# x of block 3 on loaded channel by channel: an element-wise DMA in place of transposes on TensorE

## The chip, the core and the metric

The kernel runs on one core of a Trainium2 chip. A core has TensorE (PE, the matrix engine), VectorE (DVE), ScalarE (ACT), GpSimd (POOL) and SyncE (SP, which here only issues DMAs); each runs its own instruction list in order, and they wait for one another by semaphores. Sixteen DMA engines move data between the device memory and the on-chip memory SBUF. PE writes its results to PSUM. The metric is the device time of one execution in microseconds.

## The reference

The input x has 2 x 4096 tokens of 192 channels. Three steps follow one another, and only the last result is written out.

```python
# 1: causal convolution over 7 tokens, taps = softmax(weight), one set for each of 8 heads of 24 channels
out = np.einsum('hk,bskhg->bshg', w, x_unf)          # 8192 x 192
# 2: MLP with a sigmoid GELU, 192 -> 2048 -> 192
h = x @ w_in
g = h * (1.0 / (1.0 + np.exp(-1.702 * h)))
x = g @ w_out
# 3: MLP with a rational function, 192 -> 2048 -> 192
h = x @ w_in
P = a[0] + a[1] * h + a[2] * h**2 + a[3] * h**3
Q = 1.0 + np.abs(b[0]) * np.abs(h) + np.abs(b[1]) * h**2
return (P / (Q + 1e-06)) @ w_out
```

## The kernel before

The 8192 tokens are worked on in 16 blocks of T = 512 tokens. All activations stand transposed, with channels on partitions and tokens along the free axis. Channels 0 to 127 take a block of 128 x 512; channels 128 to 191 are folded: the first 256 tokens of a block on partitions 0 to 63, the other 256 on partitions 64 to 127, in a block of 128 x 256.

A stage j overlaps three blocks: the third step of block j, the second step of block j + 1, and the preparation (convolution) of block `conv` = j + 3. Each stage has a front and a back. In the front, `front_groups` makes sixteen products of 128 hidden units each in groups of three on PE (`h_group`, lines L420 and L434); ACT reads them from PSUM (L524 is the GELU, L585 and L586 start the polynomial), VectorE goes on (L587, L588, L593, L607, and L538 for the low half of a split). L588 is the operation that lets go of a product's PSUM tile. The ring of PSUM tiles for products has three places. In the back, `back_phase` runs the second projection of block j + 1 (`o1_product`, L496 and L506), then a maximum, scales and the first products of the next front, while ACT takes logarithms and sigmoids of block j.

x comes in through three functions. `x_load` reads the rows of a block as they lie in memory, tokens on partitions, into the tile `xn` (L245, L248). `x_halo` reads the six tokens ahead of the block, element by element, straight into the transposed tile `xt` (L261 to L263). `x_transpose` turns `xn` on PE in six transposes into a PSUM tile (L272), and ACT copies that into `xt` (L278, L279). `x_red` takes the largest absolute value of `xn` on VectorE (L370), from which a power-of-two scale is made. `x_conv_pool` then convolves on POOL: seven multiplies of each part (L328) and six adds (L332). Blocks 0, 1 and 2 are prepared in a prologue and in stage 0, with the convolution as matmuls on PE; blocks 3 to 15 go by way of `back_phase` and POOL, one in each of the stages 0 to 12.

The order on each engine is that of the program text. In the front, `extras[i]` is a list of steps that are appended behind unit i; `x_red(conv)` stands in `extras[2]`, the store of block j - 1 (L626 on ACT, L630 on SP) in `extras[6]`. Since SP works in order, the loads of the next stage go out right behind that store. The scales of the third step are four tiny POOL operations (`x2_scales`, L573) that stand behind the convolution in POOL's queue, and L585 of the next front needs them. L223 copies split weights from one half of the partitions to the other, in the prologue.

Of the kernel before, what the change touches and what calls it, by code (L numbers as in the profile page):

```python
# [13 lines left out]
ALU = mybir.AluOpType  # L14
AX = mybir.AxisListType
P = 128
# [4 lines left out]
def kernel(  # L21
# [12 lines left out]
    nc = tc.nc  # L34
    B, S, D = x.shape
# [4 lines left out]
    T = 512  # L40
# [3 lines left out]
    NG = T // P  # L44
    D2 = D - P
    HALO = K - 1
    TH = T // 2
    W = T + TH
    xf = x.rearrange("b s d -> (b s) d")
# [24 lines left out]
    def ps_tile(name):  # L74
        return ps_hs[-1].tile([P, 2, 512], F32, tag="h", name=name)
# [7 lines left out]
    def all_max(red, pm):  # L83

        nc.tensor.transpose(out=pm[:, 0, 0:P], in_=red.to_broadcast([P, P]), identity=ident)
# [153 lines left out]
    xn_t, xt_t, xc_t, xs_t = {}, {}, {}, {}  # L239

    def x_load(n):

        t = p2.tile([P, W], F32, tag="xn", name="xn")
        src = xf[n * T:(n + 1) * T].rearrange("(g p) d -> p g d", p=P)
        nc.sync.dma_start(out=t[:, 0:T].rearrange("p (g d) -> p g d", g=NG), in_=src[:, :, 0:P])  # L245
        side = t[:, T:W].rearrange("p (g h d) -> p g h d", g=2, h=2)
        for h in range(2):
            nc.sync.dma_start(out=side[:, :, h], in_=src[:, 2 * h:2 * h + 2, P:D])  # L248
        xn_t[n] = t

    def x_halo(n, t=None):
# [11 lines left out]
        nc.sync.dma_start(out=t[D2:P, 0:HALO], in_=xf[first + TH - HALO:first + TH, P:D].rearrange("s d -> d s"))  # L263
        xt_t[n] = t

    def x_transpose(n):

        pt = ps_tile("pt")
        src, t = xn_t.pop(n), xt_t[n]

        def turn(dst, c):
            nc.tensor.transpose(out=dst, in_=src[:, c:c + P], identity=ident)  # L272

        for g in range(2):
            turn(pt[:, 1, g * P:(g + 1) * P], T + g * P)
        for g in range(NG):
            turn(pt[:, 0, g * P:(g + 1) * P], g * P)
        nc.scalar.activation(out=t[:, HALO:HALO + TH], in_=pt[:, 1, 0:TH], func=ACTF.Copy)  # L278
        nc.scalar.activation(out=t[:, 2 * HALO + TH:2 * HALO + W], in_=pt[:, 0], func=ACTF.Copy)  # L279
# [42 lines left out]
    def x_conv_pool(n, k):  # L322
        if k == 0:
            xc_t[n] = p1.tile([P, 2, T], F32, tag="xc", name="xc")
        c = xc_t[n]
        d = c if k == 0 else p1.tile([P, 2, T], F32, tag="tap", name="tap")
        for j, src in enumerate(x_parts(n, k)):
            nc.gpsimd.tensor_scalar(  # L328
                out=part_of(d, j), in0=src, scalar1=wt[:, j, k:k + 1], scalar2=1.0, op0=ALU.mult, op1=ALU.mult
            )  # L330
        if k:
            nc.gpsimd.tensor_tensor(out=flat_of(c), in0=flat_of(c), in1=flat_of(d), op=ALU.add)  # L332
# [24 lines left out]
    def scales(pm, dst):  # L357

        pow2_of(dst[:, 0:1], all_max_end(pm))
        nc.vector.tensor_scalar(  # L360
            out=dst[:, 1:2].bitcast(I32), in0=dst[:, 0:1].bitcast(I32), scalar1=-1, scalar2=(2 * 127 + 14) << 23,
            op0=ALU.mult, op1=ALU.add,
        )
# [3 lines left out]
    def x_red(n):  # L367

        red = red_t[n] = tiny.tile([P, 2], F32, tag="red", name="red", bufs=4)
        nc.vector.tensor_reduce(  # L370
            out=red[:, 0:1], in_=xn_t[n], axis=AX.X, op=ALU.max, apply_absolute_value=True
        )
        if n * T % S:
            nc.vector.tensor_scalar(
                out=red[:, 1:2], in0=red[:, 0:1], scalar1=red_t[n - 1][:, 0:1], scalar2=None, op0=ALU.max
            )

    def x_max(n, end=True):
        pm = pm_t[n] = ps_tile("pm")
        k = 1 if n * T % S else 0  # L380
        all_max(red_t[n][:, k:k + 1], pm)
        if end:
            x_max_end(n)
# [6 lines left out]
    def x_scales(n):  # L390
        sc = sc1_t[n]
        mul(sc[:, 3:4], sc[:, 0:1], cst[:, 0:1])
        mul(sc[:, 4:5], sc[:, 1:2], cst[:, 1:2])

    def x_scale_out(n):
        sc = sc1_t[n]
        mul(sc[:, 5:6], sc[:, 0:1], cst[:, 2:3])
        mul(sc[:, 6:7], sc[:, 5:6], cst[:, 3:4])
# [112 lines left out]
    def o1_product(part, n, i, hl):  # L511
        for k in range(2):
            f = NS * k + i
            gh, gl, wh, wl = hl[:, 0], hl[:, 1], wo1[:, f, 0:D], wo1[:, f, D:2 * D]
            part(n, f, ((wh, gh, k), (wl, gh, k), (wh, gl, k)))

    def o2_chunk(n, i, k, groups=range(NG)):
        pp = units_t[n][i][0]
        o_chunk(1, n, NS * k + i, ((pp, k, wo2[:, NS * k + i]),), groups)
# [28 lines left out]
    def x2_red_part(src, j, red):  # L548

        nc.vector.tensor_reduce(  # L550
            out=red[:, j:j + 1], in_=part_of(src, j), axis=AX.X, op=ALU.max, apply_absolute_value=True
        )
        if j:
            nc.vector.tensor_tensor(out=red[:, 0:1], in0=red[:, 0:1], in1=red[:, 1:2], op=ALU.max)
# [12 lines left out]
    def x2_scales(sc, unit):  # L567

        s = sc[:, 2:3]
        for dst, src, f in (  # L570
            (s, sc[:, 0:1], unit), (sc[:, 5:8], ab[:, 1:4], s), (sc[:, 6:8], sc[:, 6:8], s), (sc[:, 7:8], sc[:, 7:8], s)
        ):
            nc.gpsimd.tensor_scalar(out=dst, in0=src, scalar1=f, scalar2=1.0, op0=ALU.mult, op1=ALU.mult)  # L573
# [23 lines left out]
    def log(n, i):  # L597
        qq = units_t[n][i][1]
        nc.scalar.activation(out=qq, in_=qq, func=ACTF.Ln, scale=ab[:, 15:16], bias=eps)  # L599
# [11 lines left out]
    def each(f, n, steps):  # L611
        for i in steps:
            f(n, i)
# [175 lines left out]
    def x2_split(n, src, sc):  # L789
        xs = xs2_tiles(n)  # L790
        for p in (1, 0):
            high_part(src, sc[:, 1:2], xs, p)
        for p in (1, 0):
            low_part(src, sc[:, 1:2], xs, p)

    def back_phase(j, n1, n2, conv, splits):

        if conv is not None:
            x_transpose(conv)
            for k in range(K):  # L800
                x_conv_pool(conv, k)
        red = tiny.tile([P, 2], F32, tag="red2", name="red2")
        for part in (o1_main, o1_side):
            for i in range(NS):
                o1_product(part, n1, i, splits[i])
                if part is o1_main:
                    log(j, i)
            if part is o1_main:
                x2_red_part(po_t[0, n1], 0, red)
                if conv is not None:  # L810
                    x_max(conv)
                    x_scales(conv)
                    x_scale_out(conv)
        chunks = [lambda i=i, k=k: o2_chunk(j, i, k) for i in range(NS) for k in range(2)]
        each(inverse, j, (0, 1, 2, 3))
        src = po_t.pop((0, n1))
        pm = ps_tile("pm2")
        sc = sc2_t[n1] = tiny.tile([P, 24], F32, tag="sc2", name="sc2")
        x2_red_part(src, 1, red)

        def x2_ready():
            scales(pm, sc)
            x2_split(n1, src, sc)

        early[n2, 0], early[n2, 1], second[n1, 0] = h_group(
            ((0, n2, 0), (0, n2, 1), (1, n1, 0)), lambda: all_max(red[:, 0:1], pm), x2_ready
        )
        x2_scales(sc, sc1_t.pop(n1)[:, 6:7])
        each(quotient, j, (0, 1, 2, 3))
        each(inverse, j, (4, 5, 6, 7))  # L830
        for f in chunks[:3]:
            f()
        late_pe.extend(chunks[3:])
# [156 lines left out]
    with tc.manual_schedule():  # L990
        for j in range(NB - 1):
            n1, n2, conv = (j + d if j + d < NB else None for d in (1, 2, 3))
            extras = {i: [] for i in range(NS)}
            if conv is not None:
                x_load(conv)
                x_halo(conv)
                extras[2].append(lambda: x_red(conv))
            if j == 0:
                xc_t[2] = pair("pc")
                for m in range(2 * K):  # L1000
                    extras[m // 3].append(lambda m=m: x_conv_matmul(2, m))
                extras[5].append(lambda: x_high(2))
                extras[5].append(lambda: x_low(2))
            else:
                extras[NS - 2].append(lambda: store(j - 1))
                if n2 is not None:
                    extras[3].append(lambda: x_high(n2))
                    extras[4].append(lambda: x_low(n2))
            splits = (front_groups if j else front_phase)(j, n1, extras)
            if n2 is None:  # L1010
                ending(j, splits)
            else:
                back_phase(j, n1, n2, conv, splits)
# [27 lines left out]
```

## Time and profile before

| | us |
|---|---|
| median of 3 runs (1207.79 to 1208.64) | 1208.06 |
| the profiled execution | 1209.2 |
| its span, first to last instruction | 1207.2 |
| PE busy | 1181.2 (98%) |
| ACT busy | 948.1 (79%) |
| VectorE busy | 944.7 (78%) |
| POOL busy | 329.0 (27%) |

Busy times are sums of instruction durations on an engine, overlaps counted once. PE's granted clock was at its full level nearly throughout (mean 0.999). The DMA engines moved 27.86 MB, 23 GB/s on average, more than half of it in the first three of the 40 slices of the span.

### The profile page before, as it was taken

To read this page: it belongs to the slowest core of one execution; us is meant where nothing else is said; L and a number is where in the kernel's file an instruction comes from. 1 tells how busy PE (TensorE), PEld (TensorE's weight loads), DVE (VectorE), ACT (ScalarE), POOL (GpSimd) and SP (SyncE) were. 2 spreads that over 40 slices of the span, in tenths; PEclk is the share of its full clock that TensorE was granted. 3 is DMA by queue.
4 is the path that set the end of the run, shared out by engine and by line. 5 is a ranking of instruction groups with operands and counts; after the bars stand their busy time and mean duration, and the time that the engine had idled before them with its cause. 6 is when DMAs were issued, how large, how long until landed. Compare 5 with 4: busy or idle time off the path is not lost. (4 is left out here: it accounts for less than half of the span.)

```text
span 1207.2 us, 24418 instructions
## 1 busy us (share of the span) xinstructions
PE 1181.2 (98%) x10677; PEld 951.4 (79%) x10677; DVE 944.7 (78%) x1050; ACT 948.1 (79%) x969; POOL 329.0 (27%) x340
## 2 busy tenths in 40 slices
PE   9999999999999999999999999999999999999987
PEld 5547787888878788787878878787887878788677
DVE  6979787795968779596886959688695968868684
ACT  3658978779697887969788796978869788796875
POOL 0000704307071340706135080522508053000000
PEclk9999999999999999999999999999999999999999
DMA  8720001010010101001010000101001000000000
GB/s 236 228 56 1 1 1 29 1 28 1 1 28 1 27 1 27 2 1 28 1 27 2 15 14 1 27 2 27 1 1 28 2 14 1 14 1 2 14 1 27
DMA packets 55274, 27.86 MB, mean 23 GB/s; under 512 B 32896, under 2 KB 54400, under 8 KB 54400
## 3 DMA queue, kind: packets, MB, share of 16 engines
q1 hardware_dynamic: 54864, 26.31, 8.4%
q8 instruction: 83, 1.36, 0.5%
q14 instruction: 23, 0.19, 0.0%
q10 hardware_dynamic: 304, 0.00, 0.0%
HBM read 18.97 MB, written 6.29 MB: 21 GB/s over the span
## 5 line engine op out<-in xcount | busy, mean ns | idle before, releaser
L420 PE MATMUL ph<-xs,wm 128*128 128x256 f16 x3072 | 371.3, 273 | 7.3 <-ACT g L524 6.0
L420 PEld LDWEIGHTS <-wm 128*128 128x128 f16 x3072 | 292.1, 98 | 69.2 <-issue 32.2
L485 PE MATMUL po<-wo,pp 128*128 128x192 f32 x1920 | 325.6, 326 | 2.2 <-DVE pp L607 1.6
L485 PEld LDWEIGHTS po<-wo,pp 128*128 128x128 f32 x1920 | 310.1, 190 | 3.9 <-DVE pp L607 1.1
L524 ACT ACTIVATE g<-ph,sc 128x1024 f32<-128x1024 f32 x120 | 133.9, 1116 | 104.7 <-PE ph L434 104.4
L585 ACT ACTIVATE qq<-ph,sc 128x1024 f32<-128x1024 f32 x128 | 142.7, 1115 | 90.7 <-PE ph L434 51.2
L587 DVE TENSOR_TENSOR pp<-pp,ph 128x1024 f32<-128x1024 f32 x120 | 145.8, 1215 | 63.4 <-ACT pp L586 63.0
L434 PE MATMUL ph<-xs,wr 64*128 64x256 f16 x3072 | 187.0, 270 | 3.7 <-DVE hl L588 2.8
L434 PEld LDWEIGHTS <-wr 64*128 64x128 f16 x3072 | 140.6, 94 | 43.5 <-issue 22.6
L328 POOL TENSOR_SCALAR xc<-xt,wt 128x512 f32<-128x512 f32 (+1 forms) x26 | 14.9, 588 | 586.1 <-ACT xt L279 586.1
L607 DVE SCALAR_TENSOR_TENSOR pp<-pp,ab,qq 128x1024 f32<-128x1024 f32 x120 | 163.1, 1389 | 8.8 <-ACT qq L603 8.8
L593 DVE SCALAR_TENSOR_TENSOR qq<-qq,ab 128x1024 f32<-128x1024 f32 x128 | 167.2, 1307 | 0.0
L332 POOL TENSOR_TENSOR xc<-xc,tap 128x768 f32<-128x768 f32 x78 | 163.6, 2097 | 6.5
L538 DVE SCALAR_TENSOR_TENSOR hl<-g,sc,hl 128x1024 f16<-128x1024 f32 x120 | 150.1, 1280 | 14.0 <-ACT hl L534 14.0
L496 PE MATMUL po<-hl,wo 128*128 128x512 f16 x720 | 157.9, 379 | 0.0
L588 DVE SCALAR_TENSOR_TENSOR pp<-pp,sc,ph 128x1024 f32<-128x1024 f32 x120 | 153.6, 1280 | 5.3
L599 ACT ACTIVATE qq<-qq,eps,ab 128x1024 f32<-128x1024 f32 x128 | 146.8, 1228 | 0.2
L586 ACT ACTIVATE pp<-ph,sc 128x1024 f32<-128x1024 f32 x120 | 144.9, 1207 | 0.0
L496 PEld LDWEIGHTS <-wo 128*128 128x128 f16 x720 | 70.3, 98 | 82.0 <-issue 0.4
L534 ACT ACTIVATE hl<-g,sc 128x1024 f16<-128x1024 f32 x120 | 134.0, 1157 | 0.0
L328 POOL TENSOR_SCALAR tap<-xt,wt 128x512 f32<-128x512 f32 (+1 forms) x156 | 127.6, 831 | 6.4
L603 ACT ACTIVATE qq<-qq 128x1024 f32<-128x1024 f32 x128 | 124.9, 1049 | 0.2
(101 smaller groups left out, 730.2 us busy)
## 6 DMA issues: line engine op xcount, KB each, us to landing
raw<-in_moe_w_out_dram SPq DMA_DIRECT2D x8, 768.0 KB, 7.4
out_dram<-on SPq DMA_DIRECT2D x15, 384.0 KB, 2.7
xn<-in_x_dram SPq DMA_DIRECT2D x16, 256.0 KB, 3.4
raw<-in_moe_w_in_dram SPq DMA_DIRECT2D x4, 1024.0 KB, 6.0
xn<-in_x_dram SPq DMA_DIRECT2D x32, 64.0 KB, 3.0
raw<-in_moe_w_in_dram SPq DMA_DIRECT2D x4, 512.0 KB, 7.9
wr<-wr SPq DMA_DIRECT2D x8, 128.0 KB, 2.3
xt<-in_x_dram SPq DMA_DIRECT2D x30, 1.5 KB, 2.6
```

The costliest lines, as they stand in the source:

```text
L332: nc.gpsimd.tensor_tensor(out=flat_of(c), in0=flat_of(c), in1=flat_of(d), op=ALU.add)
L420: nc.tensor.matmul(out=ph[:, h, k * TH:(k + 1) * TH], lhsT=wm[m][:, a_, f], rhs=xs[:, b_, h * TH:(h + 1) * TH], start=(start and k == 0 an ...
L434: nc.tensor.matmul(out=ph[:, h, k * TH:(k + 1) * TH], lhsT=wr[m][rows, a_, other, f], rhs=xs[rows, b_, :], start=(start and other == 0 and ...
L485: nc.tensor.matmul(out=dst, lhsT=tokens(t, k, g // 2)[:, g % 2 * P:(g % 2 + 1) * P], rhs=rhs, start=(done == 0 and g % 2 == 0 and q == 0), ...
L496: nc.tensor.matmul(out=po_t[0, n][0].rearrange("p (h t) -> p h t", h=2), lhsT=w[:, 0:P], rhs=all_tokens(t, k), start=(at == 1 and q == 0), ...
L538: nc.vector.scalar_tensor_tensor(out=hl[:, 1], in0=g, scalar=sc1_t[n][:, 4:5], in1=hl[:, 0], op0=ALU.mult, op1=ALU.subtract)
L586: nc.scalar.activation(out=pp, in_=h, func=ACTF.Identity, scale=sc[:, 7:8], bias=sc[:, 6:7])
L587: nc.vector.tensor_tensor(out=pp, in0=pp, in1=h, op=ALU.mult)
L588: nc.vector.scalar_tensor_tensor(out=pp, in0=pp, scalar=sc[:, 5:6], in1=h, op0=ALU.add, op1=ALU.mult)
L593: nc.vector.scalar_tensor_tensor(out=qq, in0=qq, scalar=ab[:, 14:15], in1=qq, op0=ALU.add, op1=ALU.mult)
L599: nc.scalar.activation(out=qq, in_=qq, func=ACTF.Ln, scale=ab[:, 15:16], bias=eps)
L607: nc.vector.scalar_tensor_tensor(out=pp, in0=pp, scalar=ab[:, 0:1], in1=qq, op0=ALU.add, op1=ALU.mult)
```

## The change

For blocks 3 to 15, `x_load` and `x_transpose` are no longer called. A new function `x_turned` reads x from device memory straight into the transposed tile `xt`, with an access pattern that has channels on partitions: in eight DMAs for a block, four of 128 channels x 128 tokens and four of 64 channels x 128 tokens, in which each element of four bytes is a run of its own. `x_red` then reads `xt`, which holds the halo too, and stands in `extras[5]` instead of `extras[2]`. Blocks 0 to 2 are as before.

```diff
+    def x_turned(n):
+
+        t, first = xt_t[n], n * T
+        for g in range(NG):
+            at = 2 * HALO + TH + g * P
+            nc.sync.dma_start(
+                out=t[:, at:at + P], in_=xf[first + g * P:first + (g + 1) * P, 0:P].rearrange("s d -> d s")
+            )
+            rows, at = slice(g // 2 * D2, (g // 2 + 1) * D2), HALO + g % 2 * P
+            nc.sync.dma_start(
+                out=t[rows, at:at + P], in_=xf[first + g * P:first + (g + 1) * P, P:D].rearrange("s d -> d s")
+            )
...
-            out=red[:, 0:1], in_=xn_t[n], axis=AX.X, op=ALU.max, apply_absolute_value=True
+            out=red[:, 0:1], in_=xn_t[n] if n in xn_t else xt_t[n], axis=AX.X, op=ALU.max, apply_absolute_value=True
...
         if conv is not None:
-            x_transpose(conv)
             for k in range(K):
                 x_conv_pool(conv, k)
...
             if conv is not None:
-                x_load(conv)
                 x_halo(conv)
-                extras[2].append(lambda: x_red(conv))
+                x_turned(conv)
+                extras[5].append(lambda: x_red(conv))
```

## Rows read from the trace of the kernel before

**Rows 1.** The page, part 1: busy us (share of the span) and instructions.

```profile
PE 1181.2 (98%) x10677; PEld 951.4 (79%) x10677; DVE 944.7 (78%) x1050; ACT 948.1 (79%) x969; POOL 329.0 (27%) x340
```

**Rows 2.** Windows: one stage; length, busy us by engine, PE clock, DMA share, GB/s.

```profile
905.01:976.13 71.12, 70.65 (x668) 58.33 (x664) 55.91 (x61) 58.08 (x58) 24.78 (x24) 1.00 0.06 13
```

**Rows 3.** Waits of the whole span: total us, times, longest us.

```profile
PE ph L420 <- ACT g L524: 6.0, 13, 1.2
...
ACT qq L585 <- POOL sc L573: 25.1, 13, 2.8
...
PE ph L434 <- DVE hl L588: 2.8, 3, 1.3
```

**Rows 4.** Timeline of PE, stage 0 and a late front: start us, us, work.

```profile
104.54 1.48 PE L434 MATMUL ph<-xs,wr 64*128 64x256 f16 x24
...
968.18 2.14 PE L434 MATMUL ph<-xs,wr 64*128 64x256 f16 x36
970.25 1.48 PE L420 MATMUL ph<-xs,wm 128*128 128x256 f16 x12
...
976.34 0.88 PE L272 MATMUL pt<-ident,xn 128*128 128x128 f32 x6
977.05 10.52 PE L496 MATMUL po<-hl,wo 128*128 128x512 f16 x48
```

**Rows 5.** Timeline of VectorE, back and front of a late stage.

```profile
926.02 5.44 DVE L607 SCALAR_TENSOR_TENSOR pp<-pp,ab,qq 128x1024 f32<-128x1024 f32 x4
935.73 1.22 DVE L587 TENSOR_TENSOR pp<-pp,ph 128x1024 f32<-128x1024 f32 x1 [4.27 <-ACT pp L586]
...
954.47 0.95 DVE L370 TENSOR_REDUCE red<-xn 128x1 f32<-128x768 f32 x1
...
955.58 1.21 DVE L587 TENSOR_TENSOR pp<-pp,ph 128x1024 f32<-128x1024 f32 x1
...
966.50 1.28 DVE L588 SCALAR_TENSOR_TENSOR pp<-pp,sc,ph 128x1024 f32<-128x1024 f32 x1
...
972.30 1.22 DVE L587 TENSOR_TENSOR pp<-pp,ph 128x1024 f32<-128x1024 f32 x1
```

**Rows 6.** Timeline of ACT, back of a late stage and the next.

```profile
924.26 1.05 ACT L345 ACTIVATE xs<-po,sc 128x256 f16<-128x256 f32 x2 [0.27 <-DVE sc L360]
...
933.40 1.11 ACT L585 ACTIVATE qq<-ph,sc 128x1024 f32<-128x1024 f32 x1 [1.88 <-POOL sc L573]
...
978.55 0.38 ACT L278 ACTIVATE xt<-pt 128x256 f32<-128x256 f32 x1
978.82 0.61 ACT L279 ACTIVATE xt<-pt 128x512 f32<-128x512 f32 x1
```

**Rows 7.** Timeline of POOL: the convolutions of two stages.

```profile
926.13 4.26 POOL L328 TENSOR_SCALAR tap<-xt,wt 128x512 f32<-128x512 f32 x2
...
979.52 1.15 POOL L328 TENSOR_SCALAR xc<-xt,wt 128x512 f32<-128x512 f32 x2 [45.06 <-ACT xt L279]
...
989.02 1.82 POOL L332 TENSOR_TENSOR xc<-xc,tap 128x768 f32<-128x768 f32 x1
```

**Rows 8.** Timeline of SP: prologue, and a late stage's store and last halo.

```profile
66.18 1.27 SPq L223 DMA_DIRECT2D wr<-wr  x2
...
905.01 0.39 SPq L630 DMA_DIRECT2D out_dram<-on  x1
...
908.39 0.62 SPq L263 DMA_DIRECT2D xt<-in_x_dram  x1
```

**Rows 9.** Windows while halo elements move; columns as in rows 2.

```profile
10.00:10.20 0.20, 0.20 (x2) 0.20 (x1) 0.20 (x1) 0.10 (x1) 0.00 (x0) 1.00 1.18 8
...
109.50:109.70 0.20, 0.20 (x6) 0.14 (x6) 0.00 (x0) 0.20 (x2) 0.00 (x0) 1.00 0.60 5
...
110.80:111.50 0.70, 0.70 (x11) 0.49 (x6) 0.67 (x2) 0.70 (x1) 0.00 (x0) 1.00 0.39 3
```

## The prediction

> **What bounds the kernel now.** I began with the busy times of the page: PE is busy for 98% of the span, VectorE for 78% [rows 1]. The window of one whole stage, from one store to the next, says the same from close by: of 71.12 us PE is busy 70.65, and the DMA engines work 6% of the time [rows 2]. So a stage lasts as long as PE's instruction list plus about half a microsecond, and the change is worth what it takes off that list or adds as a wait in it. The list of waits shows that half microsecond: PE waits 13 times, once in each stage 0 to 12, for the GELU output (6.0 us), and ACT, which makes it, waited 13 times for the tiny scale operations on POOL (25.1 us) [rows 3]. For VectorE's release of PSUM PE hardly waits at all: 2.8 us in three places. Then the timelines of a late stage, engine by engine: PE, where six transposes stand between the last product of the front and the second projection [rows 4]; VectorE, which runs without a gap from 935.73 to the end of the front [rows 5]; ACT, with the two copies out of the transposes [rows 6]; POOL, whose convolution starts right after those copies, at 979.52, and whose scale operations come behind the previous one [rows 7]. Last SP, whose queue tells when x is asked for [rows 8], and the DMA windows in which nothing but four-byte elements moves, the nearest thing to the new transfers [rows 9].
>
> **What is removed.** On PE, from the first transpose (976.34) to the first matmul behind them (977.05) there are 0.71 us; the six themselves are 0.88 busy [rows 4]. They go in 13 blocks (3 to 15): 9.2 us, at most 11.4. On ACT the copies go, 0.38 + 0.61 us [rows 6]; ACT then runs eight logarithms and waits later for VectorE's scale all the same, so I count nothing for them; if ACT proved to be the bound of the back phase they would be worth up to 1 us a stage. The transposes' PSUM tile also goes, a third of the ring of three; I count nothing, since PE hardly waits for that ring.
>
> **What moves on POOL.** The convolution no longer waits for the back phase, only for x to land. If that is well before 979.5, POOL is free when the scale operations come, ACT's wait of 1.88 us in front of L585 ends [rows 6], and the following GELU is early by about that. PE's wait for it is under half a microsecond in a steady stage, so all 6.0 us of [rows 3] go.
>
> **What moves on VectorE.** The maximum over x moves from behind unit 2 to behind unit 5, that is from 954.47 to about 972.3, just ahead of L587 [rows 5], and reads the transposed tile. Its duration is the same within a tenth (780 columns for 768). Behind it in VectorE's queue stand unit 6 and the low halves of splits 6 and 7, which PE reads only some 8 us later: the products of the second projection take 10.5 us for eight splits from 977.05 [rows 4]. A late landing is thus free up to about 980, and from there PE and POOL's convolution both wait, one for one.
>
> **What is added: the transfers.** A block is 512 x 192 = 98,304 elements of four bytes, 0.393 MB, in eight DMAs behind the halos on SP. They take the place of three loads in rows. Issue costs SP some 0.6 us each [rows 8]; SP has nothing else to do until the next store, whose write queues behind them. The price is the rate. Three rows bound it [rows 9]: 8 GB/s where queued halo transfers leave only elements (10.00), 5 GB/s for a single DMA of 768 elements on idle engines (109.50), 3 GB/s for smaller ones (110.80). These give 49, 79 and 131 us a block. I take 8 GB/s: the slow rows are transfers of 24 or 48 elements per engine, in which the engines start one after another and stop again (DMA share 0.4 to 0.7), while a block gives each engine 6,144 elements without a pause, like the queued case (share 1.18). The other traffic of a stage is 13 GB/s x 71 us = 0.92 MB at a share of 0.06, or 4.3 us; without the 0.39 MB of x in rows it is some 2.5 us. So 52 us a block. Asked for at 905.4, behind the store as now, x lands about 959: 13 us before the maximum wants it and 20 before the convolution started until now. The first of these transfers can start at 66 and the convolution of block 15 began at 979.5, so DMA becomes the bound only from (979.5 - 66) / 13 = 70.3 us a block, or 5.8 GB/s.
>
> The Trainium skill speaks against this change. VectorE: DVE Perf Modes, The three transpose paths, puts a 128x128 transpose through strided DMA patterns at 19 times the 1309 ns of the hardware transpose; six such tiles would be an estimated 149 us a block, and the kernel an estimated 2.27 ms. The page speaks of large strides at the destination; here the source is strided, and the rows of this trace are faster in every window but the slowest.
>
> **What is added: contention.** The convolution now runs under the front, where VectorE is busy without a gap. Four L607 in a row took 5.44 us beside POOL, against at most 4 x 1.28 for operations of their size, and POOL's pair of multiplies took 4.26 us instead of 1.15 [rows 5, 7]. At that rate, a tenth at most, VectorE would lose 0.8 us between 959 and 966.5, where the operation that releases the last PSUM tile (unit 5) starts. PE needs that tile at 968.18 + 24/36 of 2.07 = 969.56 (the L434 take 2.07 us, until 970.25), and L588 ends at 967.78 [rows 4, 5]: 1.8 us of slack, to which come 1.1 us from the maximum that has moved behind it (955.58 - 954.47) and 1.9 from the earlier scales. So 4.8 us cover it and I count nothing; uncovered, each microsecond costs one per stage.
>
> By the Trainium skill, SBUF — State Buffer, Who interferes with whom, a VectorE operation with two SBUF inputs and a GpSimd operation that reads SBUF exclude each other for a whole instruction. VectorE could then lose up to one add of POOL, 1.82 us, at each of some four such operations before the tile is released, an estimated 7 us instead of 0.8. The trace agrees in kind, since POOL's pair was held up for 3 us, and not in size: the four L607 lost far less.
>
> **One thing at the start.** The copies of the second half of the second weights stand on SP right behind the halo of block 3 (66.18) [rows 8]. If block 3's elements get ahead of them, they land at about 118, and the product at 104.54 that first reads that half waits up to 13 us, once [rows 4]. If SP takes them first it costs nothing. I take 2.
>
> **Sum.** -9.2 (transposes) - 6.0 (GELU wait) + 2 (start) = -13.2 us against the profiled execution, which took 1209.2 us around a span of 1207.2: 1196.0. The median of the runs shown is 1.1 below that execution, so 1195. With the bounds: 11.4 + 6.0 and no loss at the start gives 1191; 9.2 alone, with 5 lost at the start, 1204.
>
> **Rivals.**
> *DMA becomes the bound; slower.* Place: the chain of transfers from 66 us on; it decides from 70.3 us a block. At 5 GB/s a block takes 78.6 + 2.5 = 81.1 us, and the span is 66 + 13 x 81.1 + 227.7 (the time from 979.5 to the end) = 1348, a run of 1349; at 3 GB/s 133.5 us a block and about 2030. For it: the only DMA of elements that ran alone shows 5 GB/s. Against: such a DMA is all start and end.
> *The convolution pushes the front.* VectorE and POOL exclude each other more than the four L607 show. It decides where VectorE loses more than 4.8 us before the release of unit 5's tile; if the 7.5 us of convolution before it were all lost, 2.7 us in 12 stages, 32 us, against a gain of 13: 1227. Against: the measured tenth.
> *The transposes were hidden anyway.* PE's 0.71 us is taken up by ACT or VectorE in the back phase, and only the start remains: 1207 to 1208. For it: ACT is without a gap there, and waits 0.27 us for VectorE's scale [rows 6]. Against: ACT loses more work than PE.
>
> **How the numbers follow.** Forecast 0.50, DMA bound 0.33, pushed front 0.12 (a quarter of it still faster, a quarter even), hidden 0.05. A difference of 0.2%, 2.4 us, is about what a measurement of this kernel can tell. Faster: 0.50 + 0.03 = 0.53; within: 0.05 + 0.03, with a little of the forecast's edge, 0.09; slower: 0.33 + 0.05 = 0.38. The likeliest case by itself lies between 1190 and 1204. Since cases of both signs hold much of the chance, the range goes from 1188 to the 5 GB/s case, 1350; beyond it lie the rates between 5 and 3 GB/s, some 0.14.
>
> **What would show it.** Right: no L272 after block 2; elements moving for about 50 us of a stage at a DMA share near 1 and 8 GB/s, then a pause until the next store; no wait of L370 for a DMA; POOL's first multiply near 959 in the stage that now starts it at 979.5, and no wait of L585 for POOL; a stage of about 69.9 us. Wrong: a DMA share near 1 through the whole stage, L370 and POOL waiting for xt from DMA, the stage as long as the transfers (rate); L434 or L420 waiting for L588 each stage, and L593, L607 and L538 well over 1.28 us (contention); a gap on PE near 105 (start).

## The result and the profile after

The changed kernel takes 1198.13 us (median of 4 runs, 1197.62 to 1198.90) against 1208.32 us for the kernel before (4 runs): a ratio of 0.9918, 95% interval 0.9902 to 0.9933, or 10.2 us less. The forecast was 1195 us with 1190 to 1204 for the likeliest case. The sign and the range held, and about three quarters of the forecast gain came. Two of the steps behind it did not hold, the start and the rate of the transfers. At the end stands a version that is 19.3 us below the kernel before.

The profiled execution took 1197.62 us around a span of 1195.9, 11.3 less than the span before. Line numbers behind the new function are 13 higher: L588 of before is L601, L585 is L598, L607 is L620, L370 is L383; the new transfers are L271 (128 channels) and L275 (64 channels). The page of after, part 1, and its DMA part:

```profile
PE 1170.9 (98%) x10599; PEld 942.8 (79%) x10599; DVE 937.7 (78%) x1050; ACT 936.0 (78%) x943; POOL 327.6 (27%) x340
...
DMA packets 1320955, 27.88 MB, mean 23 GB/s; under 512 B 1305232, under 2 KB 1320080, under 8 KB 1320080
...
q1 hardware_dynamic: 1320544, 26.32, 96.3%
q8 instruction: 83, 1.36, 0.7%
...
xt<-in_x_dram SPq DMA_DIRECT2D x52, 64.0 KB, 16.9
...
xt<-in_x_dram SPq DMA_DIRECT2D x52, 32.0 KB, 17.5
```

PE has 78 instructions less, the six transposes of 13 blocks, and its busy time is 10.3 us less [rows 1]. The bytes are the same; what is new is that nearly every packet is now a single element. The times of the packets of that queue add up to 96.3% of the span of 16 engines, against 8.4% before. That does not mean that elements move for 96% of the span: packets overlap (the DMA share below goes above 1), and the elements move for some 60 us of a stage.

**Where the time came from.** Windows of the changed kernel; the columns are those of [rows 2]. The first row is a whole stage, the next two stand in stage 0, the last three in the stage of the first row.

```profile
896.37:966.10 69.73, 69.73 (x662) 57.67 (x658) 55.75 (x61) 57.13 (x56) 24.70 (x25) 1.00 1.20 13
121.00:127.30 6.30, 0.07 (x1) 0.00 (x0) 1.82 (x4) 6.27 (x7) 1.93 (x5) 0.83 1.02 7
127.30:131.00 3.70, 3.63 (x9) 1.32 (x9) 3.66 (x5) 3.70 (x4) 3.52 (x4) 0.50 1.77 10
...
900.00:905.00 5.00, 5.00 (x24) 2.25 (x23) 3.55 (x3) 4.99 (x6) 4.82 (x4) 1.00 1.53 8
...
958.00:959.00 1.00, 1.00 (x18) 0.78 (x18) 1.00 (x2) 0.00 (x0) 0.00 (x0) 1.00 1.06 4
959.00:960.00 1.00, 1.00 (x22) 0.89 (x20) 1.00 (x2) 0.98 (x1) 0.00 (x0) 1.00 0.00 0
```

A stage is 69.73 us long and PE is busy in all of it, where it was 71.12 with 0.47 idle [rows 2]. The store of block 11 stands at 966.10 (976.13 before), that of block 0 as in these rows, the first of the kernel before, the second of the changed one:

```profile
194.12 0.39 SPq L630 DMA_DIRECT2D out_dram<-on  x1
```

```profile
199.09 0.39 SPq L643 DMA_DIRECT2D out_dram<-on  x1
```

So eleven stages take 767.01 us, where they took 782.01. That is 15.0 us won there, 1.3 more behind the last of these stores (229.8 us to the end instead of 231.1), and 5.0 lost ahead of the first: 11.3 us in all, the difference of the spans.

The timeline of PE shows the two gains and the loss. First one row of the kernel before, with the wait for the GELU, then the changed kernel:

```profile
936.75 1.47 PE L420 MATMUL ph<-xs,wm 128*128 128x256 f16 x12 [0.43 <-ACT g L524]
```

```profile
127.37 12.78 PE L509 MATMUL po<-hl,wo 128*128 128x512 f16 x48 [6.29 <-DVE xs L353]
...
925.40 2.78 PE L433 MATMUL ph<-xs,wm 128*128 128x256 f16 x24
928.11 2.14 PE L447 MATMUL ph<-xs,wr 64*128 64x256 f16 x36
...
965.54 0.83 PE L447 MATMUL ph<-xs,wr 64*128 64x256 f16 x12
966.30 6.00 PE L509 MATMUL po<-hl,wo 128*128 128x512 f16 x27
```

At 966.30 the second projection follows the last product of the front directly; the 0.71 us of [rows 4] are gone. At 925.40 the first group behind the back phase runs through its 24 matmuls without the wait for the GELU. The first row is the loss: in stage 0 PE stood 6.29 us, and then the 48 matmuls of the projection took 12.78 us instead of 10.52 [rows 4]. The granted clock in the window behind that stand is 0.50, the lower of its two levels (1.2 of 2.4 GHz), after 6.3 us in which PE was busy for 0.07.

**Why PE stood in stage 0.** The timeline of VectorE in the changed kernel, stage 0 and a late front:

```profile
125.44 0.97 DVE L383 TENSOR_REDUCE red<-xt 128x1 f32<-128x780 f32 x1 [6.35 <-DMA xt<-in_x_dram]
126.44 0.21 DVE L387 TENSOR_SCALAR red<-red 128x1 f32<-128x1 f32 x1
126.57 1.13 DVE L353 SCALAR_TENSOR_TENSOR xs<-pc,sc,xs 128x512 f16<-128x512 f32 x2
...
955.61 1.28 DVE L601 SCALAR_TENSOR_TENSOR pp<-pp,sc,ph 128x1024 f32<-128x1024 f32 x1
...
959.20 1.01 DVE L353 SCALAR_TENSOR_TENSOR xs<-xc,sc,xs 128x768 f16<-128x768 f32 x1
...
961.33 0.96 DVE L383 TENSOR_REDUCE red<-xt 128x1 f32<-128x780 f32 x1
...
965.34 2.91 DVE L551 SCALAR_TENSOR_TENSOR hl<-g,sc,hl 128x1024 f16<-128x1024 f32 x2 [0.37 <-ACT hl L547]
```

In stage 0 the maximum over block 3 (L383) waited 6.35 us for x to land. Behind it in VectorE's queue stands the low half of block 2 (L353), which PE's next work needs. In a late stage the maximum waits for nothing: x is there by 959 (the windows above), the maximum runs at 961.33. That is a margin of 2.4 us. In the eleven stages from 199.09 on the transfers end between 60 and 63.5 us behind their store, so in the tightest stage the margin is some 1.5 us.

**SP and POOL.** The timeline of SP in the changed kernel, a late store and what follows:

```profile
896.37 0.39 SPq L643 DMA_DIRECT2D out_dram<-on  x1
...
898.72 0.61 SPq L271 DMA_DIRECT2D xt<-in_x_dram  x1
899.38 8.86 SPq L275 DMA_DIRECT2D xt<-in_x_dram  x1
908.28 5.77 SPq L271 DMA_DIRECT2D xt<-in_x_dram  x1
914.09 10.04 SPq L275 DMA_DIRECT2D xt<-in_x_dram  x1
...
943.59 10.50 SPq L275 DMA_DIRECT2D xt<-in_x_dram  x1
```

Only the first transfer is issued in 0.61 us. Each later one holds SP for 4 to 11 us, and SP is free again at 954.1. A transfer of 128 channels and the one of 64 ahead of it take some 15 us together, a quarter of the time that the whole block takes; so SP probably waits until the transfers before have made room, which no run tests. The elements move from 898.7 to some 958.9, 60 us for 0.393 MB, or 6.5 GB/s.

The timeline of POOL in the changed kernel, the convolution of the same stage:

```profile
960.37 2.05 POOL L341 TENSOR_SCALAR xc<-xt,wt 128x512 f32<-128x512 f32 x2 [43.76 <-DVE xs L353]
...
984.98 0.27 POOL L586 TENSOR_SCALAR sc<-sc,sc 128x1 f32<-128x1 f32 x1
```

The convolution starts 64.0 us behind the store of 896.37; before, it started 74.5 us behind it (979.52 - 905.01) [rows 7, 8]. What released it is not the landing at 958.9 but L353, at 960.2: that step reads the previous block out of `xc`, of which there is one buffer. The scales, at 984.98, are done when ACT wants them. The list of waits of the whole span:

```profile
POOL xc L341 <- DVE xs L353: 525.2, 12, 43.8
...
DVE red L383 <- DMA xt<-in_x_dram: 6.4, 1, 6.4
PE po L509 <- DVE xs L353: 6.3, 1, 6.3
```

No wait of ACT's L598 for POOL is left in that list; [rows 3] had 25.1 us of it.

### The profile page after: what moved, and what is told of

Same layout as the page of the kernel before. It is cut to its first block, busy times and chain, and to the rows that moved or that the text cites. A ratio compares the mean times of both kernels' runs of the same rounds, so it can differ in the third digit from the quotient of the medians.

```text
span 1195.9 us, 24355 instructions
## 1 busy us (share of the span) xinstructions
PE 1170.9 (98%) x10599; PEld 942.8 (79%) x10599; DVE 937.7 (78%) x1050; ACT 936.0 (78%) x943; POOL 327.6 (27%) x340
## 3 DMA queue, kind: packets, MB, share of 16 engines
q1 hardware_dynamic: 1320544, 26.32, 96.3%
q8 instruction: 83, 1.36, 0.7%
HBM read 18.97 MB, written 6.29 MB: 21 GB/s over the span
## 4 chain that ended last, share of the span: by engine, by line
PE 90%; DVE 5%; ACT 4%; issue 1%; DMA 0%; SPq 0%; POOL 0%; ACTq 0%; DVEq 0%; POOLq 0%
PE ph L433 27%; PE po L498 26%; PE ph L447 14%; PE po L509 13%; PE po L519 7%; PE pc L331 2%; ACT qq L612 1%; DVE hl L600 0%; PE pm L85 0%; DVE wm L213 0%; DVE qq L606 0%; DVE pp L620 0%; ACT pp L599 0%; ACT hl L599 0%; ACT qq L598 0%
## 5 line engine op out<-in xcount | busy, mean ns | idle before, releaser
L598 ACT ACTIVATE qq<-ph,sc 128x1024 f32<-128x1024 f32 x128 | 142.6, 1114 | 84.8 <-PE ph L447 70.4
L341 POOL TENSOR_SCALAR xc<-xt,wt 128x512 f32<-128x512 f32 (+1 forms) x26 | 25.7, 1000 | 569.9 <-DVE xs L353 525.2
L551 DVE SCALAR_TENSOR_TENSOR hl<-g,sc,hl 128x1024 f16<-128x1024 f32 x120 | 155.7, 1326 | 12.0 <-ACT hl L547 11.9
L601 DVE SCALAR_TENSOR_TENSOR pp<-pp,sc,ph 128x1024 f32<-128x1024 f32 x120 | 153.6, 1280 | 5.3
L620 DVE SCALAR_TENSOR_TENSOR pp<-pp,ab,qq 128x1024 f32<-128x1024 f32 x120 | 149.6, 1278 | 8.8 <-ACT qq L616 8.8
L345 POOL TENSOR_TENSOR xc<-xc,tap 128x768 f32<-128x768 f32 x78 | 153.1, 1962 | 6.5
## 6 DMA issues: line engine op xcount, KB each, us to landing
xt<-in_x_dram SPq DMA_DIRECT2D x52, 64.0 KB, 16.9
```

The source lines that it names most:

```text
L341: nc.gpsimd.tensor_scalar(out=part_of(d, j), in0=src, scalar1=wt[:, j, k:k + 1], scalar2=1.0, op0=ALU.mult, op1=ALU.mult)
L551: nc.vector.scalar_tensor_tensor(out=hl[:, 1], in0=g, scalar=sc1_t[n][:, 4:5], in1=hl[:, 0], op0=ALU.mult, op1=ALU.subtract)
L601: nc.vector.scalar_tensor_tensor(out=pp, in0=pp, scalar=sc[:, 5:6], in1=h, op0=ALU.add, op1=ALU.mult)
L620: nc.vector.scalar_tensor_tensor(out=pp, in0=pp, scalar=ab[:, 0:1], in1=qq, op0=ALU.add, op1=ALU.mult)
```

## The experiments

Ten kernels. Each ratio or difference is against the kernel before, run on the same chip.

**1. The maximum of block 3 later, in stage 0 alone.** The edit, on the changed kernel:

```diff
-                extras[5].append(lambda: x_red(conv))
+                extras[5 if j else 7].append(lambda: x_red(conv))
```

> The changed kernel, with the maximum of block 3 moved behind unit 7 in stage 0; the other stages as they are. Theory: the start loses about 8 us because that maximum stands in VectorE's queue ahead of the low part of block 2, on which PE waits; with it at the end PE no longer idles there and its clock does not fall, so the run is about 1190.5 us and the first store leaves at about 192 instead of 199. Rival: the start is slow because of the transfers themselves (weight copies and elements in one queue); then moving the maximum gives back at most 1 us, 1197 or more.

Measured: 1191.73 us (1190.36 to 1192.59), ratio 0.986, interval 0.9846 to 0.9875. The windows of this kernel that answer to the stand in stage 0 and to a whole stage:

```profile
121.00:127.30 6.30, 6.30 (x31) 2.84 (x29) 6.26 (x6) 6.27 (x6) 2.86 (x4) 1.00 1.03 7
888.00:957.70 69.70, 69.70 (x660) 57.66 (x659) 55.92 (x61) 57.10 (x57) 24.66 (x25) 1.00 1.20 13
```

PE is busy in all 6.30 us, the clock stays at 1.00, the first store comes at 192.19 instead of 199.09, and the transfers are what they were. So the loss at the start was the place of one VectorE instruction, with the clock's fall on top. The two make 8.6 us in the changed kernel (6.29 and 2.26); part of that comes back, since run 1 has two waits of PE behind its projection that the changed kernel lacks (1.07 and 0.77 us).

**2. Block 3 by rows.** The edit, on the changed kernel: block 3 takes the old way, all others come by elements.

```diff
+            if conv == 3:
+                x_transpose(conv)
...
+                if j == 0:
+                    x_load(conv)
                 x_halo(conv)
-                x_turned(conv)
-                extras[5].append(lambda: x_red(conv))
+                if j:
+                    x_turned(conv)
+                extras[5 if j else 2].append(lambda: x_red(conv))
```

> The changed kernel, but block 3 comes in by rows and is transposed on PE as before; blocks 4 to 15 by elements. Theory: the loss at the start goes, and block 3's transposes come back (0.7 us): about 1191 us. Rival that the start loses to the transfers themselves: also 1191, since these are gone too; it is told apart by the run that only moves the maximum.

Measured: 1191.76 us (1189.65 to 1192.54), ratio 0.9858, interval 0.9841 to 0.9874, first store at 193.38. This is the same as run 1 within the measurement, by another way out of the same late landing.

**3. The transposes put back, unread.** The changed kernel, with the loads in rows and the six transposes on PE again; nothing reads their PSUM tile and ACT copies nothing, so only PE, PSUM, SP and the DMA engines bear them.

```diff
+    spare_t = {}
...
+            pt, rows = ps_tile("pt"), spare_t.pop(conv)
+            for g in range(2):
+                nc.tensor.transpose(out=pt[:, 1, g * P:(g + 1) * P], in_=rows[:, T + g * P:T + (g + 1) * P], identity=ident)
+            for g in range(NG):
+                nc.tensor.transpose(out=pt[:, 0, g * P:(g + 1) * P], in_=rows[:, g * P:(g + 1) * P], identity=ident)
...
+                x_load(conv)
+                spare_t[conv] = xn_t.pop(conv)
```

> The changed kernel with the row loads and the six transposes a block put back on PE, their result left unread in PSUM (no copies on ACT); the elements still come by DMA. Theory: PE is the bound in each stage, so 13 x 0.71 us come back: a stage of 70.4 us and a run of about 1207. Rival: the transposes were hidden and the gain came from the waits alone: 1198 to 1199.

Measured: 1220.17 us (1219.09 to 1222.21), ratio 1.0099, interval 1.0084 to 1.0114; more than either expected. A stage (704.33 to 775.90) takes 71.57 us with PE busy for 70.49: 0.76 more work than in the changed kernel, which is the transposes, and 1.08 of idle time that was not there. The idle time stands at one place. The timelines of this kernel, PE, VectorE and POOL in turn:

```profile
723.31 0.32 PE L85 MATMUL pm<-ident,red 128*128 128x128 f32 x1 [1.08 <-DVE red L568]
```

```profile
721.75 1.50 DVE L568 TENSOR_TENSOR red<-red 128x1 f32<-128x1 f32 x1
```

```profile
721.43 1.81 POOL L346 TENSOR_TENSOR xc<-xc,tap 128x768 f32<-128x768 f32 x1
```

L568 is the maximum of two columns, one element in a lane, between the side half of the projection and the scales. In the changed kernel it took 0.30 us; its rows, VectorE and then POOL, are these:

```profile
913.08 0.30 DVE L567 TENSOR_TENSOR red<-red 128x1 f32<-128x1 f32 x1
```

```profile
913.46 1.82 POOL L345 TENSOR_TENSOR xc<-xc,tap 128x768 f32<-128x768 f32 x1
```

There it ended 0.08 us before the add began. Here it took 1.50 us and ended at 723.25, with POOL's add (723.24). Counted from the first tap of the convolution the add begins at 22.82 us in both kernels, while the maximum begins at 22.44 us in the changed kernel and at 23.14 us here: the transposes had pushed it into the add. So the changed kernel, too, is only 0.08 us away from this wait. It is no accident of this stage: PE waited 14 times for L568, 15.3 us in all, where in the changed kernel it waited once for that step, 1.3 us. The other 13 are the stages with a convolution. Run 1 has one such place too, in stage 0, where the operation took 1.11 us and ended at 139.11 with POOL's add at 139.09. By the Trainium skill, SBUF — State Buffer, Who interferes with whom, a VectorE operation with two SBUF inputs and a GpSimd operation that reads SBUF exclude each other for a whole instruction; in these rows the two end within 0.02 us of each other.

**4. The scales on VectorE.** The kernel before, with the four scale operations taken out of POOL's queue and put on VectorE, to test the second gain by itself.

```diff
-            nc.gpsimd.tensor_scalar(out=dst, in0=src, scalar1=f, scalar2=1.0, op0=ALU.mult, op1=ALU.mult)
+            nc.vector.tensor_scalar(out=dst, in0=src, scalar1=f, scalar2=1.0, op0=ALU.mult, op1=ALU.mult)
```

> The kernel before, with the four tiny scale operations of the third step on VectorE instead of POOL, so that they no longer stand behind the convolution; transposes and loads as before. Theory: PE's wait for the GELU goes, 6.0 us in all: a stage of 70.65 us and a run of about 1202. Rival: that wait is replaced by one for VectorE or is taken up elsewhere: 1207 to 1209.

Measured: 1235.11 us (1233.46 to 1236.57), ratio 1.022, interval 1.0205 to 1.0235. The wait for the GELU is gone, and another stands in its place; PE, then VectorE, in a late stage of this kernel:

```profile
952.80 3.49 PE L485 MATMUL po<-wo,pp 128*128 128x192 f32 x20 [1.89 <-DVE pp L607]
```

```profile
949.28 0.67 DVE L573 TENSOR_SCALAR sc<-sc 128x2 f32<-128x2 f32 x2
949.86 6.38 DVE L607 SCALAR_TENSOR_TENSOR pp<-pp,ab,qq 128x1024 f32<-128x1024 f32 x4
```

The scales take VectorE from 948.42 to 949.86, and the four L607 behind them 6.38 us instead of 5.44 [rows 5]; PE waits for these, 24.2 us in 14 places, where it was 1.6 us in 2. In five of the eleven stages from 192.90 to 1000.07 PE's granted clock also falls to its lower level behind this stand: it is 0.50 from 880.50 to 882.50, after 1.9 us (876.60 to 878.50) in which PE was busy for 0.02. Behind the same stand at 950.90 it stays at 1.00. A stage with the fall takes some 74.3 us, one without it 72.6. The run tells nothing of the GELU wait; it shows that the place where the scales went was worse.

**5. The scales ahead of the last two taps.** The kernel before again, transposes and all; only POOL's order is changed, so that the scales don't stand behind the whole convolution.

```diff
         if conv is not None:
-            for k in range(K):
+            for k in range(K - 2):
                 x_conv_pool(conv, k)
...
         x2_scales(sc, sc1_t.pop(n1)[:, 6:7])
+        if conv is not None:
+            for k in range(K - 2, K):
+                x_conv_pool(conv, k)
```

> The kernel before, with the last two of the seven taps of the convolution moved behind the tiny scale operations in POOL's queue; transposes, loads and VectorE as before. Theory: PE's wait for the GELU goes and nothing takes its place: 0.4 to 0.6 us in each of 13 stages, a stage of about 70.6 us and a run of 1201 to 1203. Rival: a lock of VectorE and POOL on the memory port appears at the new place of the taps and takes the gain, 1207 or more.

Measured: 1198.91 us (1196.95 to 1202.08), ratio 0.9926, interval 0.9907 to 0.9946. This is better than expected, and as good as the change itself within the measurement. One stage of this kernel:

```profile
895.69:966.18 70.49, 70.48 (x668) 58.37 (x665) 57.54 (x61) 57.87 (x58) 24.48 (x24) 1.00 0.06 13
```

The stage takes 70.49 us, 0.63 less than before, with no idle time on PE left and the transposes still in it. So the GELU wait was worth 0.6 us a stage, and it was POOL's order that made it. The part above the expectation is at the start: the first store comes at 190.73 instead of 194.12. Of these 3.4 us the prologue gave 1.2 (stage 0's transposes start at 120.67 instead of 121.88, with no edit there); most of the rest is stage 0, where PE's wait of 1.17 us for the GELU goes, and one of 0.61 us ahead of it.

**6. The convolution of the kernel before under the front.** Transposes, copies and convolution behind unit 0, with two buffers for `xc`, so that POOL works beside VectorE's gapless stretch.

```diff
-            xc_t[n] = p1.tile([P, 2, T], F32, tag="xc", name="xc")
+            xc_t[n] = p1.tile([P, 2, T], F32, tag="xc", name="xc", bufs=2)
...
+    def x_prepare(n):
+        x_transpose(n)
+        for k in range(K):
+            x_conv_pool(n, k)
...
-            x_transpose(conv)
-            for k in range(K):
-                x_conv_pool(conv, k)
+            if j == 0:
+                x_prepare(conv)
...
-                extras[2].append(lambda: x_red(conv))
+                extras[2 if j == 0 else 0].append(lambda: x_red(conv))
+                if j:
+                    extras[0].append(lambda: x_prepare(conv))
```

> The kernel before with row loads, but the transposes and the convolution of a block put behind unit 0 of the front (stages 1 to 12) and the convolution's accumulator doubled, so that POOL runs under the part of the front in which VectorE has no gap. Theory of the forecast: VectorE loses about a tenth while POOL runs, PE does not see it, the GELU wait goes: about 1202 to 1206. Rival: VectorE and POOL exclude each other for whole instructions, VectorE loses more than 4.8 us before unit 5 lets go of its tile, a stage becomes 2 to 5 us longer: 1230 to 1270, with PE waiting for L588.

Measured: 1221.08 us (1220.63 to 1221.37), ratio 1.0108, interval 1.0091 to 1.0125. The timelines of this kernel in one front, VectorE and then PE:

```profile
962.56 2.83 DVE L607 SCALAR_TENSOR_TENSOR pp<-pp,ab,qq 128x1024 f32<-128x1024 f32 x1
965.31 1.71 DVE L593 SCALAR_TENSOR_TENSOR qq<-qq,ab 128x1024 f32<-128x1024 f32 x1
```

```profile
979.87 1.47 PE L420 MATMUL ph<-xs,wm 128*128 128x256 f16 x12 [1.47 <-DVE pp L588]
```

Single operations of 1.28 us take up to 2.83 beside the convolution, VectorE falls behind, and PE waits 1.47 us in this stage for the release of a PSUM tile, 18.6 us in 14 places over the run. Without the GELU wait the stage would be 70.5 us (run 5); with this one it is 72.01, the distance between the stores at 917.21 and 989.22. Contention under the front is real and costs 1.5 us a stage when the whole convolution runs there. Neither expectation had this size.

**7 and 8. More elements.** Run 1's kernel, with one and with two further tiles of 128 x 128 elements read in the same way in each stage from 1 on, into a tile that nothing uses: 114,688 and 131,072 elements a block for 98,304.

```diff
+    def x_extra(n, m):
+        for g in range(m):
+            t = p1.tile([P, P], F32, tag="more", name="more", bufs=2)
+            nc.sync.dma_start(out=t, in_=xf[n * T + g * P:n * T + (g + 1) * P, 0:P].rearrange("s d -> d s"))
...
+                if j:
+                    x_extra(conv, 1)
```

> The changed kernel with the maximum of block 3 moved (1191.7), and one more tile of 128 x 128 elements per block read by elements into a spare tile that nothing uses, for blocks 4 to 15. Theory: the DMA engines have some 7 us to spare in a stage of 69.7 and the tile takes 10, so they become the bound: a stage of 72 to 73 us, a run of 1218 to 1235, VectorE's maximum and POOL waiting for DMA. Rival: more elements in flight are moved faster and it stays hidden: 1192.

> The same with two more tiles per block. Theory: the stage is what the DMA engines need, 82 to 83 us, 10 us more than with one tile: a run of about 1340. Rival: a queue of more elements moves at 8 GB/s, 49 us for a block and 16 for the tiles: hidden, 1192.

Measured, in one run each: 1209.82 us and 1315.43 us. Two stages, the first of the kernel with one tile more, the second of that with two:

```profile
906.30:977.96 71.66, 69.99 (x663) 57.66 (x658) 58.16 (x60) 57.32 (x56) 27.83 (x24) 1.00 1.39 13
```

```profile
1008.98:1091.33 82.35, 72.21 (x660) 58.24 (x659) 57.37 (x61) 57.57 (x56) 27.40 (x25) 0.94 1.41 12
```

With two tiles more the transfers set the stage: the stores at 195.01 and 1091.33 are eleven stages apart, 81.5 us each, and the maximum and POOL's first tap wait for x in the stages (VectorE 122.4 us in 8 places shown as DMA, 45.5 in 3 more). 81.5 us for 131,072 elements is the same rate as 60 us for 98,304 within 2%, the halos and the store included. With one tile more the rate of the changed kernel gives 70.0 us and that of run 8 gives 71.3 us; the eleven stages of run 7 (194.72 to 977.96) take 71.2 us each. So there, too, the transfers just about fill the stage: in the stage shown the maximum waits 6.2 us for x, the convolution starts late enough to bring the GELU wait back, and PE is idle for 1.7 us. Both cost less than expected (1218 to 1235, and 1340). The prediction put the edge at 70.3 us a block; the runs bracket it, with nothing lost at 60 us, 18 us lost at some 71, and the transfers setting the stage at 81.5.

**9. The maximum back behind unit 2.** Run 1's kernel, with the other moved part undone.

```diff
-                extras[5 if j else 7].append(lambda: x_red(conv))
+                extras[2 if j else 7].append(lambda: x_red(conv))
```

> The change with the maximum of x where the kernel before has it, behind the third unit (stage 0: behind the eighth, so that the start is not disturbed). Elements land about 62.5 us after the store that they start behind, the maximum would then be wanted about 47 us after it. Theory (the move of the maximum is a needed part of the change: the transfer of 60 us does not end in time): VectorE stands some 14 us in each of 12 stages, a few of them under its slack and the work on PE's rings, so that PE waits 8 to 9 us a stage: stage 78 to 79, time 1191.7 + 12 x 8.5 = about 1290, up to 1340 where the following transfers are pushed as well. Rival (VectorE's slack and the rings in front of it swallow the wait): stage 69.73, time 1192.

Measured, in one run: 1391.94 us, 200 above run 1. VectorE, PE and the window of PE's stand in one stage of this kernel:

```profile
966.08 0.96 DVE L383 TENSOR_REDUCE red<-xt 128x1 f32<-128x780 f32 x1 [18.99 <-issue]
```

```profile
969.79 1.46 PE L447 MATMUL ph<-xs,wr 64*128 64x256 f16 x12 [16.11 <-DVE pp L601]
```

```profile
953.60:969.80 16.20, 0.09 (x4) 0.01 (x2) 3.65 (x5) 2.68 (x3) 0.00 (x0) 0.62 1.05 4
969.80:980.00 10.20, 10.20 (x67) 8.67 (x67) 10.13 (x9) 3.35 (x3) 0.00 (x0) 0.77 0.01 2
```

VectorE stood 19 us ahead of the maximum. The row says issue, which is time in which the profile shows nothing that the engine waited for. So does the list of waits in 4 of the 12 stages (72.1 us); in the other 8 it names the DMA of x (135.0 us). PE stood 16 of the 19 us, so the ring of three PSUM tiles carried it for 3 us; over the 12 stages PE stood 173.8 us, 14.5 each, where 8 to 9 had been expected. The granted clock was 0.62 over the stand and 0.77 over the next 10 us. The stores are 86.6 us apart, 16.9 more than in run 1. The place of this one instruction is worth more than everything else in the change together.

**10. A version that beats both.** Block 3 by rows (run 2), and in stage 0 alone the scales ahead of the last two taps (run 5).

```diff
-            for k in range(K):
+            for k in range(K if j else K - 2):
...
+        if j == 0:
+            for k in range(K - 2, K):
+                x_conv_pool(conv, k)
```

> Block 3 by rows, blocks 4 to 15 by elements, and in stage 0 alone the last two taps of block 3's convolution behind the four scale operations in GpSimd's queue. With block 3 by rows the first store stood at 193.38, with the same order of GpSimd's queue in the kernel by rows at 190.73 against 194.12. Theory (the two gains are independent: PE's waits of 0.58 and 1.16 us in stage 0 come from the scales behind the convolution): first store at 190 to 191, stage 69.73 as before, time 1191.8 - 2 to 3 = 1189 to 1190. Rival (GpSimd's last taps, now later, hold up the splitting of block 3 and a later unit): first store back at 193 or more, 1191.8 or above.

Measured: 1188.58 us (1187.30 to 1189.97), ratio 0.9841, interval 0.9825 to 0.9858. The first store is at 191.57, a stage 69.74, and the waits of PE for the GELU are gone from stage 0 too. It is 19.3 us below the kernel before, where the change was 10.2 below it. Run 2 was 16.9 below it, so the order of the scales gives 2.4 us more by this count and 1.8 by the first store; the ranges of the times of the two overlap, so this part is not sure to the microsecond.

## Why the prediction was right, step by step

**The transposes: right.** The prediction had 0.71 us in 13 blocks. The second projection follows directly, run 3 puts 0.76 us of work back with them, and run 5, which has everything but this, is 0.76 us a stage longer than the change. The rival that they were hidden is out.

**The GELU wait: right, and a little more.** The prediction had 6.0 us over 13 stages, 0.46 each. Run 5 shows 0.63 us a stage for POOL's order alone: the 0.47 us of idle time, and 0.17 us by which PE's busy time fell with it (70.65 to 70.48), which no run explains. The two gains together are the 1.39 us by which a stage became shorter (71.12 to 69.73); the forecast of 69.9 us was within 0.2.

**The start: wrong.** This is the step that failed: "I take 2", for weights' copies that queue behind block 3's elements. The product at 104.5 waited no longer than before (PE waits 0.8 us for those copies in both kernels). The loss came from the maximum of block 3, which the prediction had moved "from behind unit 2 to behind unit 5" with its slack worked out for a late stage only; in stage 0 the elements don't start behind a store, and the low half of block 2 stands right behind the maximum. It cost 6.9 us (199.09 against 192.19 in run 1), some 0.7 of it a prologue that happened to be longer. The landing was off too: it came at 125.3, not at 118. The lower rate and the copies that SP issued between the elements (9.7 and 9.2 us of its time) both bear on that, and no run divides the two.

**The rate: mis-sized.** The prediction had 8 GB/s, 52 us a block, and a landing 13 us before it is wanted. Measured were 6.5 GB/s, 60 us, and 2.4 us in the stage shown. The windows of 5 us between 900 and 955 still read 7 to 9 GB/s, as [rows 9] did: a window counts all that moves, and the instruction queue q8 alone has 1.36 MB in the span, 1.1 GB/s on average. So the 8 GB/s of a window of 0.2 us was probably not the elements alone; no run shows what else was in it. The error cost nothing, since the 13 us took it up; run 7 shows that a sixth more elements, 10 us, spends the margin and the gain. The mechanism, that the transfers are free up to an edge near 70 us a block and rule beyond it, agrees with runs 7 and 8. The prediction's estimate from the Trainium skill, VectorE: DVE Perf Modes, The three transpose paths, had been 149 us a block. Measured were 60 us, so the rule that spoke against the change did not decide here. All three rows of [rows 9] were faster than that estimate, the slowest (131 us) included, which the prediction leaves out.

**The move of the maximum: right, and understated.** It was told as a move that is free. Run 9 shows that it is what the change stands on: 200 us without it.

**The convolution and contention: no cost, as predicted, but not by the steps given.** The convolution was to start when x lands, 54 us behind the store. It started at 64.0, because x landed at 62.5 and L353 gave `xc` free at 63.8, a dependency that the prediction did not name. So it began only after the release of unit 5's tile (L601 ends at 956.89, 60.5 us behind the store), and the question of how much VectorE loses before that release did not arise. The operations that it makes longer (2.91 us for two L551) fall where PE waits for nothing. Run 6 shows what an earlier convolution does, 1.5 us a stage: a smaller form of the rival with the pushed front, and a reason to expect no gain from a second buffer for `xc`, which was not tried by itself.

**SP: not foreseen.** "Issue costs SP some 0.6 us each" holds for the first transfer of a block only; SP was held 55 of 70 us. It cost nothing, since the store is not due before 966.1 and SP is free at 954.1. In run 7 the issue of the store itself was held, 8.26 us at 906.30.

**The sum: right in part by luck.** Behind the first store 16.3 us were won, where 15.2 had been forecast for all stages together; ahead of it 5.0 were lost, where 2 had been forecast. The two errors have opposite signs. And that the range allowed for 5 us at the start is luck too, since it allowed them for another cause.

## What to carry to other kernels

When a load becomes slow, look first at the in-order queue of the engine that consumes it: with the maximum behind unit 5 the same 60 us transfer cost nothing in a late stage and 6 to 7 us in stage 0, and with it behind unit 2 it cost 200 us over the run. Work the slack out for the first and the last stage too, not only for the steady one. And test a gain that comes from an order (the scales behind the convolution) by the order alone: here it gave 8.4 us, 1.2 of them from a prologue that it does not touch, where the whole change gave 10.2, and it needs no new transfer.

## What the runs showed of the hardware

- Elements of four bytes with channels on partitions, on 16 engines: 98,304 took 60 us in the stage shown, and 131,072 took 81.5 us a stage in run 8. That is 16 x 60 us / 98,304, some 10 ns for each element and engine, over the whole transfer.
- The engine that issues such transfers (here SP) was itself held: 0.6 us for the first of a block, 4 to 11 us for each from the second on.
- A VectorE operation on one column took 0.30 us or 1.50 us, by whether POOL's add was running; with the add it ended when the add did. Six transposes on PE, 0.76 us of work, were enough to put it there in 13 stages (run 3).
- After a stand of 6.3 us PE's granted clock was 0.50, and the projection behind it took 12.78 instead of 10.52 us. In run 9, after a stand of 16 us, the clock was 0.77 on average over the next 10 us. In these places a long wait on PE cost more than its own length.
